# A fused convolution and SwiGLU kernel: weights held back by one DMA, the first output stage reordered, one late sum moved from POOL to an adding DMA, the last pair's products reordered

## The chip, the cores and the metric

The kernel runs on one core of one Trainium2 chip. The metric is the device time of one execution in microseconds (us). The kernel before took 2653.93 us, the median of three runs (2653.21 to 2660.86).

The engines are named as the profile names them: PE is TensorE (matmuls), PEld its weight loads, DVE is VectorE, ACT is ScalarE, POOL is GpSimd, and SP is SyncE, which only issues DMAs. A DMA can also be issued from ACT or from POOL; one from POOL may add to what stands at its destination.

## The reference

The input x has 8 sequences of 4096 tokens with 192 channels, in 8 heads of 24. Each head has 7 taps, made by a softmax over its weights, and every token becomes the tapped sum of itself and the six tokens before it. The 32768 results go through a SwiGLU block:

```
out  = einsum('hk,bskhg->bshg', softmax(weight), windows of x)   # causal, 7 taps per head
rms  = sqrt(mean(x*x) + 1e-6)                                    # x: the result above, 32768 x 192
xn   = x / rms * rms_g
g    = xn @ w_gate          # 192 x 1536
val  = xn @ w_val           # 192 x 1536
y    = (silu(g) * val) @ w_out   # 1536 x 192
```

The weights w_gate, w_val, w_out and rms_g come as 64-bit floats and are read as pairs of 32-bit words; the kernel turns them into 32-bit floats itself.

## The kernel before, in words

**Pairs.** The tokens go in 32 pairs of two tiles of 512 tokens (PT = 1024, T = 512). Pair 0 is computed plainly. Pairs 1 to 31 use a scheme that computes products of 3 by 3 blocks with 15 block products in place of more, so that TensorE has fewer products and the other engines have sums to form. For every pair there are 120 products of the first matrices (line 859: gate on the low 64 partitions, value on the upper 64, four units u of 384 columns each, in chains that accumulate in the eight PSUM banks), and then 60 products of the last matrix (line 1044, each four 32-column matmuls), listed in OUTS as form.unit: 11.0 is form 11 of unit 0.

**Order.** Everything is issued in an order written out by hand. ORDER is a list of steps for one pair: `p3` is three products of TensorE; every other word has the engine as its first letter (V for DVE, A for ACT, G for POOL, P for DVE again, Q for a DMA from POOL, D for a DMA from SP) and then the step. A name that ends in `-` belongs to the pair before. Each engine takes its steps in that order and waits where a semaphore tells it to. A later scheduler does not move them.

**Sums of a pair.** The gated results of a unit are six tiles a to f in the tile `ht`. The output products read them and sums of them: AB, CB, X and S, held in `early`, `more`, `nt` and `tls`. The method `Pair.sum` (line 1059) forms them. A word such as `Gabe.13` adds e to AB for the units 1 and 3 on POOL, in one instruction over both units (line 1062); `Qbe.2` adds e to b for unit 2 by a DMA from POOL that accumulates (line 1082); single units on POOL or DVE are at line 1084; `k` before the name copies an operand into a PSUM bank first (line 765). The sum be is written into b itself, and the products of form 1 read it. AB has three states in a pair: form 8 reads AB as it is, form 13 reads it after abe, form 2 after abd. So a sum has to wait until the products of the state before have been read.

**The next pair's input.** While a pair runs, the convolution, the norm (square, reduce, power, repeat, spread, scale: lines 495 to 560), the stores of the normed rows to DRAM in another layout (`place`, line 682), the fetch of them as operands (fetB, fetA, fetC: lines 713 and 736) and the sums of operands (`x_sum`, lines 750 and 757, and the swaps of halves, line 722) of the pairs behind are done in its gaps. Between fetB and fetA a one-element DMA called mark (line 733) reads what fetB has written, so SP waits there until fetB has landed.

**The start.** The input block of pair 0 (x0) is loaded by SP, and the weights behind it. So that the weights do not take transfer time from x0, `hold` (line 224) and two further lines (151, 1315) copy the last loaded column of x0 on POOL into the tiles that the weights will fill; each weight DMA has to wait for its tile's copy. rms_g (rg_sb) is loaded behind the first weights. `convert` turns the words into floats; its last step for the input weights multiplies by rg_sb (line 346), and the first products of pair 0 (line 1168) wait for that. START gives the order of pair 0's steps by one letter each, LATER the time slots of the rest.

**The first output stage.** Pair 0's last matrix is done plainly (`outer`, line 1209, 384 matmul records), in four groups of banks; ACT copies one half of a group (line 1217) and DVE adds the other (line 1221). In its gaps, by numbers of a planned clock (`put(base + ...)`: these give an order, not a time), the kernel does the norm multiply of pair 1 (line 551), its placing and fetch, seven operand sums on DVE (line 757), 17 weight sums for the units 2 and 3 (`w_sums`, line 372), two sign changes of weights on ACT (`w_signs`, line 381), 17 sums of output weights (`out_sums`, line 945), and the norm of pair 2 with the power of its factors on POOL (line 517).

**The last pair.** It has nothing behind it to prepare. The function `last` sorts its steps: each late step (a fork, a join J, a transpose T, a store st) is put in as soon as the names that NEEDS lists for it are done.

```
    NEEDS = {
        "D6": "F4 S6", "D0": "S8 F0", "D2": "S2 F4", "D3": "S2 F3", "D1": "S5 F1",
        "D13": "S13 S6", "D7": "S7 S6", "T0": "3 D0", "T1": "10 D1", "T2": "1 D13 D7",
        "T3": "14 D3", "T4": "0 F4", "T5": "F4 D2 D6", "st0": "T0 T1 T2", "st1": "T3 T4 T5",
        "S2": "2",
    }
```

Of the kernel before, what the change touches and what calls it, by code (L numbers as in the profile page):

```python
# [19 lines left out]
def kernel(  # L20
# [10 lines left out]
    nc = tc.nc  # L31
# [115 lines left out]
    def load_heads(p, b, t0):  # L147

        t = x_sb[p] = xs.tile([P, TB + HALO, GS], F32, name="xh")
        if p == 1:  # L150
            nc.gpsimd.tensor_copy(out=t[:, 0, 0:1], in_=x0[:, NJ + HALO - 1, 0:1])

        def get(dst, tb, h, dims, r):
            row = x[b, t0 + tb * TB + r - HALO, h * GS :]
            src = bass.AP(
                tensor=row.tensor, offset=row.offset, ap=[dims, [D, TB + HALO - r], [1, GS]]
            )
            nc.sync.dma_start(out=dst, in_=src)
# [65 lines left out]
    def hold(t):  # L224

        if 0 in x_sb:
            nc.gpsimd.tensor_copy(out=t, in_=x_sb[0][:, NJ + HALO - t.shape[1] :, 0])

    ht4 = big.tile([P, NU, 2, NF, T], F32, name="ht")

    def load_in(u, q):
        cols = slice(u * NF * P, (u + 1) * NF * P)
        t = ht4[:, u].rearrange("p a f t -> p (a f t)")[:, 0 : KP * NF * P * 2].bitcast(U32)
        t = raw["in", u] = t.rearrange("p (k n two) -> p k n two", k=KP, two=2)
        hold(t[:, :, 0, 0].bitcast(F32))
# [16 lines left out]
    def load_out(i):  # L252


        if i < 2:
            t = outs.tile([P, T // P, D], F32, name="o_sb")
            t = t[:].rearrange("p j d -> p (j d)")
            hold(t[:, 0 : PF * D * 2 : D * 2])
# [8 lines left out]

    load_in(0, nc.sync)
# [111 lines left out]
    def w_signs():  # L380
        nc.scalar.mul(wf4[:, :, 6:9:2, :], wf4[:, :, 6:9:2, :], -1.0)
# [296 lines left out]
    def place(p):  # L678
# [9 lines left out]
        for first in range(2) if p == 1 else (0,):  # L688
            q = nc.scalar if first else nc.sync
            for h in range(first, H, 2 if p == 1 else 1):  # L690
                q.dma_start(out=to[h], in_=y[h::H])
            yield
# [35 lines left out]
    def fetch_part(p, act):  # L728
# [3 lines left out]
        if (p, 1 - g) in fetched:  # L732
            nc.sync.dma_start(out=mark[:, 0:1], in_=xb[HP : HP + 1, 1 - g, 0, 0:1])
# [246 lines left out]
    class Pair:  # L980
# [48 lines left out]
        def products(self):  # L1029
# [4 lines left out]
            for w in " ".join(OUTS).split():  # L1034
# [24 lines left out]
        def sum(self, name, us, eng):  # L1059
            if len(us) > 1:  # L1060
                dst, a, b = (self.forms(i, [int(u) for u in us]) for i in SUMS[name])
                nc.gpsimd.tensor_tensor(out=dst, in0=a, in1=b, op=ALU.add)  # L1062
                return
# [220 lines left out]
    def done(it):  # L1284
# [11 lines left out]
        "iwpvsicwpsiwvpisvivcpsocvpwispvswcipvwsipsiwOvpsiwvipsvvpsopsvcpsvOnovoOpsonvOpsnoOvnopso"  # L1296
    )
    LATER = (
        (30, "s"), (35, "v"), (45, "v"), (47, "O"), (50, "O"), (53, "O"), (55, "n"), (60, "t"),
# [15 lines left out]
    nc.gpsimd.tensor_copy(out=rg_sb[:, 0:1], in_=x0[:, NJ + HALO - 1, 0:1])  # L1315
# [36 lines left out]
    put(base + 445, functools.partial(next, pieces["t"], None))  # L1352
# [28 lines left out]
    emit(float("inf"))  # L1381
# [11 lines left out]
    def last(order, outs):  # L1393

        got, row, n = set(), [], 0
        ends = {w.split(".")[0]: i for i, w in enumerate(outs)}
        late = [w.strip("-") for w in order if w.strip("-")[1:] in NEEDS]
        for w in order:
            if w[-1] == "-":
                row.append(w)  # L1400
                continue
            if w[1:] in NEEDS:
                continue
            for w in ["p1"] * int(w[1:]) if w[0] == "p" else [w]:
                row.append(w)
                if w[0] != "p":
                    got.add(w[1:])
                else:
                    n += 1
                    got.update(k for k, i in ends.items() if i + 121 == n)  # L1410
                more = True
                while more:
                    more = [w for w in late if got.issuperset(NEEDS[w[1:]].split())]
                    for w in more[:1]:
                        late.remove(w)
                        row.append(w)
                        got.add(w[1:])
# [48 lines left out]
```

## Time and profile before

| What | Value |
| --- | --- |
| Time, median of three runs | 2653.93 us (2653.21 to 2660.86) |
| Profiled execution | 2659.7 us, span of its instructions 2657.8 us |
| Granted TensorE clock in it | 0.997 |
| Busy share of the span: PE, DVE, POOL, ACT | 98%, 90%, 81%, 73% |
| First product of pair 0 (L1168) | starts at 34.49 us |
| First fast pair (first L859 product to the next pair's) | 89.5 us |
| A later pair, the same | 80.9 us |
| Sums of two units on POOL: be (L1062, ht) | 31, mean 2.67 us |
| Adding DMAs from POOL (L1082) | 124 of 256 KB, four a pair |

How to read the lines that follow in the next part: the page gives for every engine its busy time, its share of the span and its number of instructions, then the DMA queues with packets, megabytes and share, then the chain of work that ended last by engine. A row of waits says which engine and line waited for what, how long in total, how often, and the longest. A row of the order of time has the start, the duration, engine, line, operation, what is written and read, its shape, the number of instructions merged into the row, and in brackets the idle time before with what ended it. A row of landings has what is written and read, the queue, the number, the size and the time from issue to landing.

### The profile page before, as it was taken

Reading aid. Unit: us, or ns where it says so; the run is one execution under the profiler, and the core shown is the slowest. Engines: PE = TensorE matmul, PEld = TensorE weight load, DVE = VectorE, ACT = ScalarE, POOL = GpSimd, SP = SyncE. Lnnn points to the kernel's source line nnn. Section 1 sums busy time; section 2 is a strip of 40 time slices with the busy share of each in tenths; the row PEclk is TensorE's granted clock in tenths of the full one; section 3 lists DMA queues with packets and bytes.
Section 4 is the critical chain, followed back from the end, with each engine's and each line's share of the span. In section 5 each row is a group of like instructions: output and inputs, shape, how many; then the busy total and the mean of one; then the engine's idle time right before and its main releaser. Section 6 shows DMA issues by size and latency. Waiting matters only on the chain.

```text
span 2657.8 us, 61651 instructions
## 1 busy us (share of the span) xinstructions
PE 2592.4 (98%) x23128; PEld 1617.2 (61%) x23128; DVE 2388.9 (90%) x3989; ACT 1951.2 (73%) x3779; POOL 2156.8 (81%) x1439
## 2 busy tenths in 40 slices
PE   8999999999999999999999999999999999999998
PEld 6856566665566665566655666655666556665555
DVE  7879999999999999999999999999999999998976
ACT  5577777877777877777877778777787777787765
POOL 4777789877789777898777897777897778987777
PEclk9999999999999999999999999999999999999999
DMA  6333443434453434444344534344434444343331
GB/s 141 72 72 73 87 94 84 84 73 86 80 101 75 86 69 91 86 88 80 74 86 80 101 79 85 68 95 80 94 74 84 75 86 95 83 85 68 78 73 29
DMA packets 520345, 218.67 MB, mean 82 GB/s; under 512 B 456174, under 2 KB 458734, under 8 KB 520046
## 3 DMA queue, kind: packets, MB, share of 16 engines
q1 hardware_dynamic: 500044, 181.63, 34.0%
q0 software_dynamic: 17856, 32.51, 7.1%
q8 instruction: 182, 2.98, 0.5%
q14 instruction: 117, 0.96, 0.1%
q10 hardware_dynamic: 2146, 0.59, 0.1%
HBM read 100.10 MB, written 49.55 MB: 56 GB/s over the span
## 4 chain that ended last, share of the span: by engine, by line
PE 58%; POOL 26%; issue 6%; DVE 5%; ACT 3%; DMA 1%; SPq 0%; DVEq 0%; POOLq 0%; ACTq 0%
PE ps L859 49%; POOL early L1062 8%; PE ps L1044 6%; POOL ht L913 3%; POOL xa L750 3%; POOL nt L1062 3%; PE ps L1168 2%; POOL ht L1062 2%; POOL nt L1084 2%; POOL early L1082 1%; ACT ps L765 1%; DVE early L1084 1%; POOL ht L1082 1%; DVE tile L893 1%; POOL tls L1084 1%
## 5 line engine op out<-in xcount | busy, mean ns | idle before, releaser
L859 PE MATMUL ps<-xa,wf 64*128 64x512 f32 x7440 | 1633.2, 592 | 7.7 <-DMA xa<-xa 3.6
L859 PEld LDWEIGHTS ps<-xa,wf 64*128 64x128 f32 x7440 | 1045.9, 187 | 581.6 <-issue 281.5
L811 ACT ACTIVATE tile<-ps 128x512 f32<-128x512 f32 (+1 forms) x801 | 449.2, 573 | 194.3 <-PE ps L1044 107.1
L811 ACT ACTIVATE ps<-ps 128x512 f32<-128x512 f32 x744 | 401.2, 553 | 138.7 <-PE ps L1044 92.4
L811 ACT ACTIVATE tls<-ps 128x512 f32<-128x512 f32 (+1 forms) x656 | 361.5, 565 | 172.2 <-PE ps L1044 88.5
L913 POOL TENSOR_TENSOR ht<-ht,tile 128x512 f32<-128x512 f32 x310 | 414.4, 1347 | 64.9 <-ACT tile L905 61.6
L913 POOL TENSOR_TENSOR ht<-ht,tls 128x512 f32<-128x512 f32 x248 | 329.8, 1344 | 82.2 <-ACT tls L905 81.5
L1044 PE MATMUL ps<-ht,x 128*32 128x256 f32 x5952 | 396.4, 379 | 0.1
L481 DVE SCALAR_TENSOR_TENSOR ps<-xh,tp,ps 128x512 f32<-128x512 f32 x450 | 326.0, 750 | 3.9 <-ACT ps L473 1.7
L1044 PEld LDWEIGHTS ps<-ht,x 128*32 128x32 f32 x5952 | 198.6, 110 | 123.2 <-issue 7.8
L1044 PE MATMUL ps<-early,x 128*32 128x256 f32 x3968 | 255.7, 381 | 12.8 <-POOL early L1062 12.8
L1062 POOL TENSOR_TENSOR early<-early,ht 128x1024 f32<-128x1024 f32 (+1 forms) x93 | 267.3, 2968 | 0.4 <-PE ps L1044 0.4
L531 POOL TENSOR_TENSOR r<-r,nhalf 128x8 f32<-128x8 f32 x29 | 48.2, 1662 | 266.8 <-ACT r L527 257.5
L893 DVE TENSOR_TENSOR tile<-ps,tile 128x512 f32<-128x512 f32 x341 | 233.0, 685 | 12.2 <-PE ps L859 8.0
L893 DVE TENSOR_TENSOR ht<-ps,tile 128x512 f32<-128x512 f32 x316 | 214.0, 682 | 0.7
L905 ACT ACTIVATE tile<-tile 128x512 f32<-128x512 f32 x341 | 211.9, 627 | 0.0
L893 DVE TENSOR_TENSOR tls<-ps,tls 128x512 f32<-128x512 f32 x279 | 190.2, 685 | 11.4 <-PE ps L859 6.0
L1044 PEld LDWEIGHTS ps<-early,x 128*32 128x32 f32 x3968 | 123.1, 110 | 116.8 <-POOL early L1062 42.5
L765 ACT COPY ps<-ht 128x512 f32<-128x512 f32 x279 | 164.2, 589 | 35.3 <-DVE early L1084 33.2
L905 ACT ACTIVATE tls<-tls 128x512 f32<-128x512 f32 x279 | 172.6, 626 | 0.0
L1084 DVE TENSOR_TENSOR early<-early,ps 128x512 f32<-128x512 f32 x217 | 142.9, 682 | 31.4 <-PE ps L1044 31.3
L893 DVE TENSOR_TENSOR ht<-ps,tls 128x512 f32<-128x512 f32 x242 | 163.2, 682 | 1.7 <-ACT tls L811 1.2
(172 smaller groups left out, 3698.8 us busy)
## 6 DMA issues: line engine op xcount, KB each, us to landing
xa<-xd SPq DMA_DIRECT2D x120, 384.0 KB
xa<-xa SPq DMA_DIRECT2D x124, 256.0 KB
out_dram<-o_sb SPq DMA_DIRECT2D x246, 96.0 KB
xd<-yn SPq DMA_DIRECT2D x244, 96.0 KB
xh<-in_x_dram SPq DMA_DIRECT2D x192, 105.0 KB
xa<-xd SPq DMA_DIRECT2D x68, 256.0 KB
ht<-ht POOLq DMA_DIRECT2D x62, 256.0 KB, 3.9
nt<-ht POOLq DMA_DIRECT2D x31, 256.0 KB, 3.3
```

Of the source, the lines that this page charges most:

```text
L481: nc.vector.scalar_tensor_tensor(out=dst, in0=xk, scalar=w, in1=at, op0=ALU.mult, op1=ALU.add)
L750: nc.gpsimd.tensor_tensor(out=put[0], in0=put[1], in1=put[2], op=ALU.add)
L765: nc.scalar.copy(out=bank(*at)[:], in_=src)
L811: nc.scalar.activation(out=dst, in_=src, func=AF.Copy, scale=float(s))
L859: nc.tensor.matmul(out=self.new(v, h, True) if first else self.old(v, h), lhsT=wf[self.u][HALF[h], WAT[i], :], rhs=x_op(XOP[i], h), start= ...
L893: nc.vector.tensor_tensor(out=dst, in0=self.old(v, h), in1=t[:], op=plus(s))
L905: nc.scalar.activation(out=t[:], in_=src[:], func=AF.Silu)
L913: engine[eng].tensor_tensor(out=self.hv(v), in0=src, in1=t[:], op=ALU.mult)
L1044: nc.tensor.matmul(out=to[q * Q : (q + 1) * Q, :], lhsT=left[:, u, a], rhs=cols[:, i * HALFT : (i + 1) * HALFT], start=fresh, stop=True, s ...
L1062: nc.gpsimd.tensor_tensor(out=dst, in0=a, in1=b, op=ALU.add)
L1082: nc.gpsimd.dma_start(out=dst, in_=b, accum_op=ALU.add)
L1084: engine[eng].tensor_tensor(out=dst, in0=a, in1=b, op=ALU.add)
```

## The change

It has six parts, and none changes the number of matmuls.

1. *Start.* `hold` and the two further POOL copies go. One DMA, `begun`, writes the last loaded column of x0 to DRAM from SP's queue. It waits for x0, and what stands behind it in SP's queue waits with it. In the order that the program gets, the first two loads of gate weights stand ahead of `begun`, the others behind.
2. *First output stage.* The norm multiply of pair 1 goes from LATER into START, ahead of the last two conversions of output weights on POOL. `place` issues all its stores from SP, for pair 1 too. The seven operand sums of pair 1 go from DVE to POOL, as three double sums and one single, and stand there behind three sums of output weights and four weight sums; the swaps follow them. The power of pair 2's norm stands on POOL behind all 17 weight sums and ahead of the last fourteen sums of output weights, which stood ahead of it. `w_signs` is done in two halves, for the units 0 and 1 where it was, for 2 and 3 later.
3. *fetA.* The marker DMA is left only where fetB comes second, which the order does not have. So it goes.
4. *be.13.* The word `Gbe.13` becomes `Qbe.13`: b += e for the units 1 and 3 by one adding DMA of 512 KB in place of one POOL instruction. `Pair.sum` gets the branch for it.
5. *Last pair's products.* In the last pair the products of form 0 are sorted behind all others.
6. *Last pair's steps.* `last` is written anew to follow that order: a step whose needs are met is put in before the products of form 0. With this order the products 2.2, 2.3 and 2.1 of the last pair are issued ahead of the sums abd.23 and abd.1, which change what they read: these products of this one pair are formed from AB without d, and the two sums wait for the products.

```
-        "Acv0_2 Gp9.23 DfetA Vcv1_0 Pp9.1 p1 Qbe.2 p1 Vcv2_0 AF1 p2 Gbe.13 DfetC p2 Vcv1_2 Vcv3_0",
+        "Acv0_2 Gp9.23 DfetA Vcv1_0 Pp9.1 p1 Qbe.2 p1 Vcv2_0 AF1 p2 Qbe.13 DfetC p2 Vcv1_2 Vcv3_0",
...
-        if p == 1:
-            nc.gpsimd.tensor_copy(out=t[:, 0, 0:1], in_=x0[:, NJ + HALO - 1, 0:1])
...
-    def hold(t):
-
-        if 0 in x_sb:
-            nc.gpsimd.tensor_copy(out=t, in_=x_sb[0][:, NJ + HALO - t.shape[1] :, 0])
...
+    begun = dram.tile([P, 1], F32, name="begun")
+    nc.sync.dma_start(out=begun[:], in_=x0[:, NJ + HALO - 1, 0:1])
     load_in(0, nc.sync)
...
-        for first in range(2) if p == 1 else (0,):
-            q = nc.scalar if first else nc.sync
-            for h in range(first, H, 2 if p == 1 else 1):
-                q.dma_start(out=to[h], in_=y[h::H])
-            yield
+        for h in range(H):
+            nc.sync.dma_start(out=to[h], in_=y[h::H])
+        yield
...
-        if (p, 1 - g) in fetched:
-            nc.sync.dma_start(out=mark[:, 0:1], in_=xb[HP : HP + 1, 1 - g, 0, 0:1])
+        if g == 0 and (p, 1) in fetched:
+            nc.sync.dma_start(out=mark[:, 0:1], in_=xb[HP : HP + 1, 1, 0, 0:1])
...
-            for w in " ".join(OUTS).split():
+            outs = " ".join(OUTS).split()
+            if self.p == PAIRS - 1:
+                outs.sort(key=lambda w: w[0:2] == "0.")
+            for w in outs:
...
-                nc.gpsimd.tensor_tensor(out=dst, in0=a, in1=b, op=ALU.add)
+                if eng == "Q":
+                    nc.gpsimd.dma_start(out=dst, in_=b, accum_op=ALU.add)
+                else:
+                    nc.gpsimd.tensor_tensor(out=dst, in0=a, in1=b, op=ALU.add)
...
-        "iwpvsicwpsiwvpisvivcpsocvpwispvswcipvwsipsiwOvpsiwvipsvvpsopsvcpsvOnovoOpsonvOpsnoOvnopso"
+        "iwpvsicwpsiwvpisvivcpsocvpwispvswcipvwsipsiwOvpsiwvipsvvpsopsvcpsvOnovoOpsonvOpsnoOvnnopso"
...
-    later(norm(2), c + 1510, c + 1600, c + 2310, base + 2895, base + 2900)
+    later(norm(2), c + 1510, c + 1600, c + 1610, base + 2895, base + 2900)
...
-    for i, at in zip(range(4), (1660, 1730, 2060, 2130)):
-        put(c + at, functools.partial(x_sum, i))
-    put(c + 2131, functools.partial(swap, "swA"))
-    for i, at in zip((5, 4, 6), (2200, 2270, 2290)):
-        put(c + at, functools.partial(x_sum, i))
-    put(c + 2291, functools.partial(swap, "swB"))
+    for at, i in zip((470, 471, 473, 474), (20, 21, 4, 22)):
+        put(base + at, functools.partial(x_sum, i, "G"))
+    put(base + 472, functools.partial(swap, "swA"))
+    put(base + 475, functools.partial(swap, "swB"))
     wsum = out_sums()
-    later(wsum, *[base + 964 + 60 * i for i in range(17)])
-    put(base + 2650, w_signs)
+    later(wsum, *[base + 455 + i for i in range(3)], *[base + 2100 + 60 * i for i in range(14)])
+    put(base + 2650, functools.partial(w_signs, 0, 2))
...
+    put(base + 3595, functools.partial(w_signs, 2, 4))
```

More of the change, by code (lines that the diff above doesn't have):

```diff
@@ L234, in load_in @@
         t = raw["in", u] = t.rearrange("p (k n two) -> p k n two", k=KP, two=2)
-        hold(t[:, :, 0, 0].bitcast(F32))
         for w, rows in ((moe_w_gate, LOW), (moe_w_val, UPP)):
@@ L257, in load_out @@
             t = t[:].rearrange("p j d -> p (j d)")
-            hold(t[:, 0 : PF * D * 2 : D * 2])
         else:
@@ L378, in w_sums, with w_signs @@
         yield
-    def w_signs():
-        nc.scalar.mul(wf4[:, :, 6:9:2, :], wf4[:, :, 6:9:2, :], -1.0)
+    def w_signs(lo, hi):
+        t = wf4[:, lo:hi, 6:9:2, :]
+        nc.scalar.mul(t, t, -1.0)
     def convert_in(u):
@@ L1295 @@
         "XxxxxxxXdDdDdDddTTTTTTTTaakKkkaaakKkKbkKkbKbbbffpffpfsipsvivpsipisvipsvcpvowsivOcwps"
-        "iwpvsicwpsiwvpisvivcpsocvpwispvswcipvwsipsiwOvpsiwvipsvvpsopsvcpsvOnovoOpsonvOpsnoOvnopso"
+        "iwpvsicwpsiwvpisvivcpsocvpwispvswcipvwsipsiwOvpsiwvipsvvpsopsvcpsvOnovoOpsonvOpsnoOvnnopso"
     )
     LATER = (
-        (30, "s"), (35, "v"), (45, "v"), (47, "O"), (50, "O"), (53, "O"), (55, "n"), (60, "t"),
+        (30, "s"), (35, "v"), (45, "v"), (47, "O"), (50, "O"), (53, "O"), (60, "t"),
         (463, "w"), (564, "w"), (664, "w"), (764, "w"), (864, "w"),
@@ L1314 @@
     conv_first((1, 3, 5, 6), 2)
-    nc.gpsimd.tensor_copy(out=rg_sb[:, 0:1], in_=x0[:, NJ + HALO - 1, 0:1])
     nc.sync.dma_start(out=rg_sb[LOW, :], in_=rg)
@@ L1351 @@
     put(base - 1, lambda: outer(0, hts, base))
-    put(base + 445, functools.partial(next, pieces["t"], None))
     put(base + 450, functools.partial(fetch, 1))
@@ L1393, in last, with settle, product @@
     def last(order, outs):
-        got, row, n = set(), [], 0
-        ends = {w.split(".")[0]: i for i, w in enumerate(outs)}
+        got, row, n, end = set(), [], 0, []
+        todo = [w.split(".")[0] for w in outs]
         late = [w.strip("-") for w in order if w.strip("-")[1:] in NEEDS]
+        def settle():
+            more = True
+            while more:
+                more = [w for w in late if got.issuperset(NEEDS[w[1:]].split())]
+                for w in more[:1]:
+                    late.remove(w)
+                    row.append(w)
+                    got.add(w[1:])
+        def product(k):
+            row.append("p1")
+            todo.remove(k)
+            if k not in todo:
+                got.add(k)
+            settle()
         for w in order:
@@ L1400, in last @@
                 row.append(w)
[L1401 to L1404, printed above, removed]
-                row.append(w)
[L1406 to L1417, printed above, removed]
+            elif w[0] == "p":
+                for _ in range(int(w[1:])):
+                    n += 1
+                    k = outs[n - 121].split(".")[0] if n > 120 else ""
+                    if k == "0":
+                        end.append(k)
+                    elif k:
+                        product(k)
+                    else:
+                        row.append("p1")
+            elif w[1:] not in NEEDS:
+                row.append(w)
+                got.add(w[1:])
+                settle()
+        for k in end:
+            product(k)
         assert not late
```

## The prediction

> **What bounds the kernel now.** I read the page first (busy shares, chain), then the waits, then the order of time of three places that the change touches: the first 36 us, the hand-over from the first output stage to the first fast pair (92 to 145 us), and one later pair (868 to 950 us), with the transfers of that pair.
>
> ```profile
> span 2657.8 us, 61651 instructions
> PE 2592.4 (98%) x23128; PEld 1617.2 (61%) x23128; DVE 2388.9 (90%) x3989; ACT 1951.2 (73%) x3779; POOL 2156.8 (81%) x1439
> ...
> q8 instruction: 182, 2.98, 0.5%
> ...
> PE 58%; POOL 26%; issue 6%; DVE 5%; ACT 3%; DMA 1%; SPq 0%; DVEq 0%; POOLq 0%; ACTq 0%
> ```
>
> TensorE is bound nearly everywhere: 98% busy, and 31 pairs follow each other every 80.9 us (first L859 product to first L859 product). The 26% of POOL in the chain are POOL's sums late in each pair, which arrive just as TensorE wants them. The start (the chain in order of time, then the waits):
>
> ```profile
> 2.33 6.32 DMA x<-in_x_dram
> ...
> 8.81 7.71 POOL ht L227
> ...
> 27.81 5.97 DMA rg_sb<-in_moe_rms_g_dram
> ```
> ```profile
> PE ps L1168 <- DVE wf L346: 5.5, 1, 5.5
> ...
> DVE wf L346 <- DMA rg_sb<-in_moe_rms_g_dram: 5.2, 1, 5.2
> ```
>
> The input block is in at 8.65, but the POOL copy that holds the weights back runs from 8.81 to 16.5, exactly as long as VectorE's tap products; the weights start then, rg_sb stands behind them in the queue and lands at 33.8, and TensorE's first product waits for it. The hand-over (order of time of PE, then of DVE):
>
> ```profile
> 136.17 2.59 PE L859 MATMUL ps<-xa,wf 64*128 64x512 f32 x6 [3.63 <-DMA xa<-xa]
> 141.28 51.48 PE L859 MATMUL ps<-xa,wf 64*128 64x512 f32 x230 [2.52 <-DVE o_sb L1221]
> ```
> ```profile
> 140.54 0.24 DVE L543 STREAM_TRANSPOSE s<-s 128x64 f32<-128x64 f32 x1 [8.51 <-POOL s L520]
> 140.71 0.52 DVE L1221 TENSOR_TENSOR o_sb<-ps,o_sb 128x384 f32<-128x384 f32 x1
> ```
>
> Two waits, for the swapped sums and for the last bank, which stands on VectorE behind a transpose that waits for POOL's power. A later pair (POOL, then PE, then the landings):
>
> ```profile
> 928.45 0.86 POOL L1082 DMA_DIRECT2D ht<-ht  x1
> 929.06 2.67 POOL L1062 TENSOR_TENSOR ht<-ht 128x1024 f32<-128x1024 f32 x1
> 931.38 1.18 POOL L1082 DMA_DIRECT2D early<-ht  x1
> 932.34 6.07 POOL L1062 TENSOR_TENSOR early<-early,ht 128x1024 f32<-128x1024 f32 x2
> ```
> ```profile
> 934.19 0.61 PE L1044 MATMUL ps<-ht,x 128*32 128x256 f32 x8
> 935.04 1.50 PE L1044 MATMUL ps<-early,x 128*32 128x256 f32 x24 [0.23 <-POOL early L1062]
> ...
> 938.46 0.64 PE L1044 MATMUL ps<-early,x 128*32 128x256 f32 x8 [0.19 <-POOL early L1062]
> ```
> ```profile
> ht<-ht POOLq DMA_DIRECT2D x1, 256.0 KB, 3.8
> early<-ht POOLq DMA_DIRECT2D x1, 256.0 KB, 3.6
> ```
>
> The row at 929.06 is the sum be.13, which the change hands to an adding DMA; the row at 934.19 is product 1.1, the first reader of its result; 935.04 is 13.1, 938.46 is 7.3.
>
> **The change part by part.** *Start.* The four POOL copies go (and those for rg_sb and xh); one small DMA (begun) waits on SP for the input block, which landed at 8.65. Two gate transfers now stand ahead of it in SP's queue. The other weights start at about 9 instead of 17, so rg_sb lands about 8 us earlier, near 25.5. VectorE's step ahead of L346 ended at 28.82, so L346 starts at 28.9 instead of 33.99: -5.1. All engines' later work hangs on L346 and moves with it. Bounds: not over 5.5 (the whole wait of PE); if the two gate transfers (384 KB at the 225 KB per us that the packets show here) ran ahead of the input block they would cost 1.7, leaving -3.4. They stand behind it in the queue, so I take -5.1.
>
> *First output stage* (before's times, all less 5.1). The norm multiply L551 moves from 107.0 to 101.0; its 2.9 us cover POOL's wait of 1.9 at 105. The eight stores of y now all go on SP (5.2 us, as at 143.78) and start at 104 instead of 110 on two queues; the eight fetches follow from 109.3 instead of 114.1, and as they are bound by transfer rate (1.16 us each in the landings), the sixth lands near 118.5, the last near 121. POOL: last conversion ends 108.1, three output sums 3.0, four weight sums 3.1, to 114.2; it then waits for the fetch until 118.5; three double sums (2.58 each, L750) and one single (1.5) to 127.7; the last swap is issued there instead of at 131.6 and lands 4.45 later, at 132.2: the wait of 3.63 goes. What is late next: thirteen weight sums (0.77 each, 10.0) and the power with its copies (2.35) end at 140.1; the transpose and the last L1221 behind it end near 140.9 instead of 141.2. So -0.3: POOL spends on waiting and on sums that VectorE did before (7.7 us) what it saves on the fourteen output sums put behind (12.4). The split w_signs stands ahead of the last L1217 on ACT and waits for the thirteen, to 137.7; L1217 ends by 139.2, ahead of 140.9. Bounds: -6.1 if both waits went, +3 if the fetch is as late as before.
>
> *Behind it.* Fourteen sums and the second norm multiply now end at 155.4 instead of 143.75, so the first M multiply, which ran at 150.24, ends at 156.7. The snapshot L815 at 156.00 takes the tile that it frees: 0.7 late, and product (4,5) waits for that. POOL was idle 6 us between 150 and 168 and catches up. +0.7 (0 to 2.3).
>
> *Every pair, mark.* The marker DMA goes; SP issues fetA when the last product has read its place, 1.4 us earlier. Nothing on the path waits for fetA. 0.
>
> *Every pair, be.13* (31 times). POOL loses 2.67 and gains an issue of about 1. That is no gain: abe.13 behind it must wait for product 8.1, whose end reached POOL at 932.27 in the record; it started 0.07 later. The transfer: 256 packets of 2 KB, 16 to each of 16 engines, behind the 8 of Qbe.2 in the same queue. Qbe.2's packets ran from 929.85, 0.187 us each; 24 in a row end at 934.35, and POOL's transfers land 0.33 after their last packet: 934.7. 1.1 would start at 934.76, 0.57 late. 13.1 is then 0.2 late; 7.3 waited 0.38 for its sum anyway and abd.23, which holds 2.2, has another 0.15. So a clean landing costs nothing, and each us beyond 934.8 costs one.
>
> It will seldom be clean. The instruction queue's 182 packets of 16 KB took 0.5% of 16 engines' span, 1.17 us each on one engine; by the packet records one starts within 60.3 to 66.2 us of the pair in 30 of 31 pairs, just where this transfer runs. Qabe.2, half as long, landed at 3.6 (median), but 0.5 to 2.0 later in 9 pairs, mean 1.3. I take 1.0 late: (934.7 + 1.0 + 0.07 + 0.46) - 935.04 - 0.53 = 0.65 a pair, times 31 = +20. Bounds: 0 (clean) and 2.0 late, 1.6 a pair, +50. POOL's issue of twice the descriptors is not in the trace; between 0.86 and 1.7 it stays hidden, since Qabe.2 has to wait for 8.2 (about 930.9).
>
> The Trainium skill, page "DMA: Bandwidth & Descriptors", section "Anatomy of one DMA — SWDGE (gpsimd) path", fits such a DMA as 2.0 us plus bytes over 436 GB/s; by that 512 KB would take 3.2 us and land at 932.3, ahead of 1.1, and the sum would be without the 20. The trace has 3.6 to 3.8 for 256 KB where the page gives 2.6, so I go by the rows.
>
> *Last pair.* Products 0.x come last, so T5, T3, T0 and store st0 run beside four products; behind the last product only T4 and st1 are left, two transposes (0.37 each) fewer. -0.8 (0 to -1.7, four products of 0.43).
>
> Sum: -5.1 - 0.3 + 0.7 + 20 - 0.8 = +14.5. The profiled execution took 2659.7 (span 2657.8 and 1.9 around it), so 2674.2 against it; it stands 5.8 above the median of the runs, 2653.9 (2653.2 to 2660.9). Against the median: 2668.4.
>
> **The rivals.** *The transfer is in time* (not slower): be.13 lands by 934.8 in most pairs, since only one of 16 engines is held by a code packet and fetA's earlier issue clears the queue. Then the twenty are gone: 2648.4. For it: 0.53 us of slack behind 1.1. Against: Qbe.2 itself landed 4.1 after issue in the median, not 3.3, and 1.1 needs every engine. It decides at a landing 5.7 us after issue. *The first output stage gains as well*: if POOL's sums run faster or the fetch lands earlier, so that neither wait is left: -5.1 - 5.8 - 0.8, and a hidden transfer: 2642.2. Against: thirteen weight sums stand ahead of the power. *The transfer is later still*: descriptors of two rows a partition, or adds that share the engines with fetch traffic, add 2 us more than a clean landing: +50, 2698. *Only the start moves* and the rest cancels is the first rival's time.
>
> **How the numbers follow.** Forecast 0.55, in time 0.27, stage gains too 0.08, later still 0.10. The forecast's own range is 2655 to 2685 (0.2 to 1.2 a pair). Within 0.3% (8 us, what a measurement here can tell from no change) are the first rival and the lower part of the forecast, 0.10: 0.37; faster 0.08; slower 0.55. The range leaves the second rival below and most of the third above: 2645 to 2692.
>
> **What would show it.** PE's first L1168 product at 29.4; no wait for xa<-xa, and the next pair's period still near 89 with the last L1221 held by POOL; POOL's L1062 on ht replaced by a DMA; a new wait of PE at a product of ht for a DMA, 0.5 to 1.6 us, about 31 times, and a period of 81.5 instead of 80.9. Wrong if the period stays at 80.9 (landing early, or more slack than I found), or if abe.13 starts earlier (then 8.1 was not what held it).

## The result, and the profile after

The kernel after takes 2663.82 us (median of 20 runs, 2662.68 to 2668.21); the kernel before took 2654.19 us beside it (20 runs, 2652.58 to 2662.21). The ratio is 1.0031, with a 95% interval of 1.0025 to 1.0038: slower by about 0.3%, 8 us. The medians are 9.6 apart; six of before's runs lie near 2660, so that its mean, 2656.0, stands above its median. The forecast was 2668.4. The sign and the size came out, but two large terms of the sum were wrong by +10 and by -15 us and hid each other, so most of what follows is on why.

One sentence of the section on the change is wrong: the products 2.2, 2.3 and 2.1 of the last pair are not issued ahead of abd.23 and abd.1. They stand behind these sums in the new order too, and in the trace abd.23 ends 1.2 us ahead of product 2.2. Nothing is left out of the computation.

The page of the kernel after, its span and the chain by engine (DMA was 1% of it before):

```profile
span 2663.0 us, 61597 instructions
...
PE 2587.8 (97%) x23128; PEld 1607.5 (60%) x23128; DVE 2381.6 (89%) x3982; ACT 1948.9 (73%) x3780; POOL 2120.3 (80%) x1437
...
PE 60%; POOL 19%; DMA 7%; DVE 6%; issue 5%; ACT 2%; SPq 0%; POOLq 0%; DVEq 0%; ACTq 0%
```

The start, from the chain in order of time (start, duration, what):

```profile
2.33 7.55 DMA x<-in_x_dram
...
10.02 7.79 DMA begun<-x
...
17.83 9.75 DMA o_sb<-in_moe_w_out_dram
...
27.59 5.43 DMA rg_sb<-in_moe_rms_g_dram
```

The input block lands at 9.88, where it landed at 8.65 before. The DMA begun needs 7.8 us to land, a weight transfer that waits for its completion 9.75, and rg_sb is issued at 27.59, where it was issued at 27.81 before. PE's first product of pair 0 starts at 33.66.

The hand-over to the first fast pair (order of time of PE):

```profile
132.48 1.22 PE L851 MATMUL ps<-xa,wf 64*128 64x512 f32 x4 [1.08 <-DMA xa<-xa]
136.94 2.07 PE L851 MATMUL ps<-xa,wf 64*128 64x512 f32 x2 [3.24 <-ACT o_sb L1215]
140.68 2.08 PE L851 MATMUL ps<-xa,wf 64*128 64x512 f32 x4 [1.67 <-DVE o_sb L1219]
```

There are three waits instead of two. The one for the swapped sums is shorter (1.08, was 3.63), the last bank still waits for VectorE, and between them stands a new one for ACT's last copy.

The later pairs, from the waits (who waited for what: us in total, times, longest) and the landings of POOL's DMAs, then one pair in the order of time of POOL and of PE:

```profile
PE ps L1039 <- DMA ht<-ht: 30.4, 31, 1.6
...
ht<-ht POOLq DMA_DIRECT2D x62, 256.0 KB, 3.5
ht<-ht POOLq DMA_DIRECT2D x31, 512.0 KB, 6.3
```
```profile
930.86 1.54 POOL L1058 DMA_DIRECT2D ht<-ht  x1
933.08 0.91 POOL L1080 DMA_DIRECT2D early<-ht  x1 [0.67 <-PE ps L1039]
934.17 5.80 POOL L1060 TENSOR_TENSOR early<-early,ht 128x1024 f32<-128x1024 f32 x2 [0.18 <-PE ps L1039]
```
```profile
937.66 0.64 PE L1039 MATMUL ps<-ht,x 128*32 128x256 f32 x8 [1.46 <-DMA ht<-ht]
938.12 1.48 PE L1039 MATMUL ps<-early,x 128*32 128x256 f32 x24
```

This pair starts 1.78 us later than the pair shown of before, so the row at 934.17 (abe.13) is where it was, 64.1 us into its pair. Product 1.1, at 937.66, waits 1.46 for the 512 KB transfer.

Where the time went, by stretches, with the start of each stretch read from PE's rows. The column in the middle is the kernel before with the last pair's edits alone (a run told below); up to the last pair it does the same work as before:

| Stretch, us | before, the profiled run | before's work, another run | after |
| --- | --- | --- | --- |
| to the first product of pair 0 | 34.49 | 28.47 | 33.66 |
| from there to the first fast pair | 96.92 | 96.70 | 96.61 |
| first fast pair | 89.49 | 90.06 | 91.85 |
| pairs 2 to 30 (29 pairs) | 2348.52 | 2349.31 | 2352.47 |
| last pair to the end | 88.41 | (edited) 87.46 | 88.42 |

The first row is the surprise: before has two kinds of start, 6.0 us apart. Its 20 runs show them as two groups, 14 from 2652.6 to 2655.8 and 6 from 2660.2 to 2662.2, and the profiled run (2659.7) was of the rarer kind. Five traces have the start of after, with the first product between 33.66 and 34.71. Against the usual start, after loses 5.2 at the start, 0 to the first fast pair, 1.8 in it, 3.2 in the pairs 2 to 30, and with 88.41 for the last pair of before nothing at the end: 10.1 in all, where the medians differ by 9.6.

### The profile page after: what moved, and what is told of

Its sections match the earlier page's. It is cut to its first block, busy times and chain, and to the rows that moved or that the text cites. A ratio compares the mean times of both kernels' runs of the same rounds, so it can differ in the third digit from the quotient of the medians.

```text
span 2663.0 us, 61597 instructions
## 1 busy us (share of the span) xinstructions
PE 2587.8 (97%) x23128; PEld 1607.5 (60%) x23128; DVE 2381.6 (89%) x3982; ACT 1948.9 (73%) x3780; POOL 2120.3 (80%) x1437
## 4 chain that ended last, share of the span: by engine, by line
PE 60%; POOL 19%; DMA 7%; DVE 6%; issue 5%; ACT 2%; SPq 0%; POOLq 0%; DVEq 0%; ACTq 0%
PE ps L851 48%; PE ps L1039 8%; POOL early L1060 6%; DMA ht<-ht 5%; POOL ht L905 4%; POOL xa L742 3%; PE ps L1166 2%; POOL nt L1060 2%; POOL nt L1082 2%; DVE ps L475 1%; PE ps L1207 1%; DMA xa<-xd 1%; POOL xa L749 1%; POOL tls L1082 1%; ACT ps L803 1%
## 5 line engine op out<-in xcount | busy, mean ns | idle before, releaser
L851 PEld LDWEIGHTS ps<-xa,wf 64*128 64x128 f32 x7440 | 1033.9, 187 | 594.9 <-issue 298.6
L1060 POOL TENSOR_TENSOR early<-early,ht 128x1024 f32<-128x1024 f32 (+1 forms) x93 | 253.9, 2739 | 6.2 <-PE ps L1039 6.2
L1039 PEld LDWEIGHTS ps<-early,x 128*32 128x32 f32 x3968 | 129.7, 110 | 84.5 <-POOL early L1060 1.5
```

The costliest lines, as they stand in the source:

```text
L851: nc.tensor.matmul(out=self.new(v, h, True) if first else self.old(v, h), lhsT=wf[self.u][HALF[h], WAT[i], :], rhs=x_op(XOP[i], h), start= ...
L1039: nc.tensor.matmul(out=to[q * Q : (q + 1) * Q, :], lhsT=left[:, u, a], rhs=cols[:, i * HALFT : (i + 1) * HALFT], start=fresh, stop=True, s ...
```

## The experiments

Each kernel was run beside the kernel before on the same chip; ratios are to that.

| Run | Median, us | Ratio to before (95%) |
| --- | --- | --- |
| after, be.13 back on POOL | 2660.93 | 1.0017 (1.0009 to 1.0026) |
| after, begun of one element | 2659.46 | 1.0013 (1.0004 to 1.0022) |
| before, last pair's edits alone | 2654.41 | 1.0000 (0.9991 to 1.0009) |
| the same, T3 behind form 0 | 2653.59 | 0.9997 (0.9988 to 1.0006) |
| before, first output stage's edits alone | 2656.05 | 1.0003 (0.9994 to 1.0012) |
| after, power ahead | 2667.21 | 1.0045 (1.0031 to 1.0059) |
| after, power ahead and backlog spread | 2659.28 | 1.0015 (1.0006 to 1.0023) |
| the four mended together | 2646.47 | 0.9967 (0.9955 to 0.9980) |
| before, be.13 as a DMA alone | 2676.22 | 1.0070 (1.0056 to 1.0083) |
| mended, be.13 as a DMA ahead of be.2 | 2642.10 | 0.9949 (0.9936 to 0.9961) |
| before, rg_sb early | 2655.86 | 1.0001 (0.9992 to 1.0010) |
| after, the marker back | 2678.93 | 1.0083 (1.0070 to 1.0097) |

**be.13 put back.**

```
-        ... Qbe.2 p1 Vcv2_0 AF1 p2 Qbe.13 DfetC ...
+        ... Qbe.2 p1 Vcv2_0 AF1 p2 Gbe.13 DfetC ...
```

> The kernel after with the sum be.13 put back on POOL, all else as after. Theory (the late landing costs, but most of it is eaten by slack: in the two traces the pairs 2 to 31 took 3.95 us more in all, the first pair some 0.6): 4 to 5 us faster than the kernel after, 2659 to 2660 us, every period between 80.86 and 80.97, no wait for a DMA at a product of ht. Rival 1 (the adding DMA explains the whole loss, because it also disturbs other transfers): 8 to 10 us faster, 2654 to 2656. Rival 2 (the adding DMA is harmless and the periods of after are noise of that one run): 2663 to 2665, periods still spread over 80.6 to 82.2.

Measured: 2660.93, 2.9 us faster than after by the medians, and about 3.7 by the ratios (1.0017 where after has 1.0031), a little under the 4 to 5 expected. In the traces the pairs 2 to 30 took 2348.76 in all, as before (2348.52), the last pair 87.75 instead of 88.42 and the first fast pair 91.45 instead of 91.85. So in the kernel after the adding DMA costs 0.4 + 3.7 + 0.7 = 4.8 by the traces. The first fast pair stays long, so all but 0.4 of its 1.8 is not the DMA's.

**begun of one element.**

```
-    begun = dram.tile([P, 1], F32, name="begun")
-    nc.sync.dma_start(out=begun[:], in_=x0[:, NJ + HALO - 1, 0:1])
+    begun = dram.tile([1, 1], F32, name="begun")
+    nc.sync.dma_start(out=begun[:], in_=x0[P - 1 : P, NJ + HALO - 1, 0:1])
```

> The kernel after with begun reading and writing one element instead of 128. Theory (the 128 writes of 4 bytes to DRAM hold the DMA engines: behind them weight packets of 3 KB took up to 6.9 us instead of 0.24, from 11 to 20 us, so the weights and rg_sb came no earlier than before): the weight packets behind begun take 0.2 to 0.4 us again, rg_sb is issued near 21.5 instead of 27.6, the first product of pair 0 (L1166) starts at 29.0 to 30.0 instead of 33.66, and the whole is 3.7 to 4.7 us faster than the kernel after, 2659 to 2660. Rival (it is only the wait of the queue for any DMA's completion, or the weights wait for something else): the first product stays between 32 and 34, the time within 1.5 us of the kernel after.

Measured: 2659.46; the first product starts at 27.89, 5.8 earlier than in after, rg_sb is issued at 18.16 and 18.86. The busy time by stretch shows what the weights waited for (last columns: granted clock, DMA share, GB/s), first after, then this run:

```profile
10.00:12.00 2.00, 2.00 (x16) 2.00 (x16) 1.94 (x6) 2.00 (x7) 0.00 (x0) 1.00 1.80 26
12.00:16.00 4.00, 4.00 (x29) 4.00 (x29) 4.00 (x14) 4.00 (x12) 0.00 (x0) 1.00 0.72 24
16.00:20.00 4.00, 3.69 (x28) 3.52 (x27) 2.34 (x8) 2.31 (x6) 0.00 (x0) 1.00 0.47 28
```
```profile
10.00:12.00 2.00, 2.00 (x14) 2.00 (x13) 2.00 (x7) 2.00 (x7) 0.00 (x0) 1.00 0.94 244
12.00:16.00 4.00, 4.00 (x29) 4.00 (x28) 4.00 (x14) 4.00 (x13) 0.00 (x0) 1.00 1.03 220
16.00:20.00 4.00, 3.56 (x26) 3.09 (x24) 2.08 (x6) 2.82 (x8) 0.00 (x0) 1.00 1.08 288
```

Behind 128 writes of 4 bytes the engines moved 24 to 28 GB/s for ten microseconds, where behind one write they moved 220 to 288. By the packet records 38 of the weights' packets of 3072 bytes took over 1 us in after (up to 6.9; the median is 0.23), none here; all 38 start between 11.7 and 19.1, behind begun's issue. But the edit changes the order of SP's queue as well. In after two gate loads are issued ahead of begun, in this run none (SP, first after, then this run):

```profile
3.09 1.21 SPq L230 DMA_DIRECT2D ht<-in_moe_w_gate_dram  x2
10.02 0.37 SPq L260 DMA_DIRECT2D begun<-x  x1
```
```profile
8.33 0.22 SPq L260 DMA_DIRECT2D begun<-x  x1
8.60 1.84 SPq L230 DMA_DIRECT2D ht<-in_moe_w_gate_dram  x3
```

In after the packets of these two loads start at 6.68, while the input block is still coming in, and begun is issued 1.7 us later than here. So the run shows that begun's shape and the two loads ahead of it lost the start together. The slow packets stand for the shape as the larger part; no run has the one without the other. That the queue then also waited 3.4 us for begun's completion is not parted from this either: with one element that wait is gone too. The specifications of the Trainium skill's page "DMA: Bandwidth & Descriptors" name 512 bytes as the least size for full rate, with a read, change and write back below it; the traces agree in sign, and no run here shows that mechanism.

**Last pair's edits alone, and with T3 behind the products of form 0.**

```
             outs = " ".join(OUTS).split()
+            if self.p == PAIRS - 1:
+                outs.sort(key=lambda w: w[0:2] == "0.")
...
(second run only)
-        "T3": "14 D3", "T4": "0 F4",
+        "T3": "14 D3 0", "T4": "0 F4",
```

> The kernel before with the last pair's edits alone (the products of form 0 sorted last, the function last rewritten). Theory (the four products of form 0 write the half of a PSUM bank whose other half the transpose T3 reads, and T3 now stands ahead of them; PE waited 1.78 us there in the kernel after): the same wait of 1.5 to 2 us at the last four products for a transpose on DVE, from the last pair's first product to the end of the span 88.3 to 88.6 us as before (88.41), time within 0.5 of the kernel before. Rival (the edit gains as forecast, and in the kernel after be.13 ate it): 87.5 to 87.7 us for the last pair, 0.8 faster.

> The kernel before with the last pair's edits, and with the transpose T3 put behind the products of form 0 (one name more in its list of needs), so that nothing reads their bank ahead of them. Theory (the bank is what holds them): no wait of PE at the last four products, last pair 1.0 to 1.6 us shorter than with the edits alone (the last product ends 1.78 earlier, one transpose of 0.37 and its half of the stores come back behind it), so 86.9 to 87.4 us. Rival (DVE's joins and transposes end last in any case): less than 0.4 us shorter.

Measured: 2654.41 and 2653.59, no difference that a run's time could tell, but in the traces the last pair takes 87.46 and 86.92 instead of 88.41. PE at the last four products, first run and second run:

```profile
2645.55 1.93 PE L1047 MATMUL ps<-ht,x 128*32 128x256 f32 x32 [1.78 <-DVE o_sb L1060]
```
```profile
2644.47 1.93 PE L1047 MATMUL ps<-ht,x 128*32 128x256 f32 x32 [0.54 <-DVE ps L1109]
```

The wait for the shared bank is there as expected, but it does not eat the gain: the edit saves 0.95, because behind the last product only one transpose and half of the stores are left. So my theory fell and the rival held: the edit gains, and in the kernel after the late be.13 took 0.67 of it (87.75 with be.13 on POOL). T3 moved is worth 0.54, about half of the least that I expected: PE still waits 0.54 there for a join of VectorE on the same bank, and a transpose and its half of the stores come back behind the products.

The first of these two traces also shows the other start. The order of time of POOL and of VectorE at the start, of this run, and then of the kernel before as profiled:

```profile
8.56 0.34 POOL L227 COPY ht<-x 128x3 f32<-128x3 f32 x1 [7.01 <-DMA x<-in_x_dram]
```
```profile
8.99 7.33 DVE L434 SCALAR_TENSOR_TENSOR y<-x,taps,y 128x192 f32<-128x192 f32 x22
```
```profile
8.81 7.71 POOL L227 COPY ht<-x 128x3 f32<-128x3 f32 x1 [7.26 <-DMA x<-in_x_dram]
```
```profile
9.14 7.33 DVE L434 SCALAR_TENSOR_TENSOR y<-x,taps,y 128x192 f32<-128x192 f32 x22
```

The same POOL copy takes 0.34 us or 7.71. In four traces with this code it ended before VectorE's first L434, and the weights started between 8.5 and 9.3; in two it came back only when L434's series was over, and the weights started at 16.5. The lead alone does not part them: it was 0.27 and 0.33 us where the copy lost, 0.31 to 0.56 where it won. What decides is not shown.

**The first output stage: its edits alone, the power moved, the backlog spread.**

```
(on after, second and third run)
-        (463, "w"), (564, "w"), (664, "w"), (764, "w"), (864, "w"),
+        (463, "w"), (1820, "w"), (1821, "w"), (1822, "w"), (1823, "w"),
...
-    put(base + 3595, functools.partial(w_signs, 2, 4))
(second run only)
+    put(base + 9000, functools.partial(w_signs, 2, 4))
(third run only: signs, norm multiply, placing and six output sums go into pair 1's order)
-    later(wsum, *[base + 455 + i for i in range(3)], *[base + 2100 + 60 * i for i in range(14)])
+    later(wsum, *[base + 455 + i for i in range(3)], *[base + 464 + i / 2 for i in range(8)])
...
+    EXTRA = {
+        "GM3.1.0": [more_sum] * 4, "Gac.0": [more_sum] * 2,
+        "AS41.1.1": [functools.partial(w_signs, 2, 4)],
+        "Gmul-": [functools.partial(next, norm2, None)], "Dplace-": [functools.partial(done, place(2))],
+    }
```

> The kernel before with the edits of the first output stage alone. Theory (the stage gains nothing by itself, and the first fast pair is 1.2 us longer because TensorE's products run at half speed for 5.3 us after the three waits instead of 2.7 after the two of before): first product to the first fast pair as before within 0.3, the first fast pair 91.0 to 91.6 instead of 89.5 to 90.0, whole 1 to 2 us slower than before. Rival (the first pair is longer because of the adding DMA be.13 or the late start): 89.5 to 90.1, no slower.

> The kernel after with the power of the second norm ahead of the thirteen weight sums on POOL, and the second half of the sign changes behind ACT's last copy of the stage. Theory (PE waits for the last bank only because VectorE's and ACT's last copies stand behind a transpose and sign changes that wait for these sums; but POOL has the same work to do, so its first multiply of the pair stays at 153, and a tile that it frees is needed 14.7 us after PE resumes): PE resumes at 132.5 to 134 instead of 140.7, and most of that is given back by a new wait of 4 to 7 us in the first fast pair; whole 0 to 4 us faster than the kernel after. Rival (POOL's backlog is hidden): 8 to 9 us faster.

> As the run with the power moved, and POOL's backlog moved too: eight of the fourteen late output sums into POOL's wait for the fetch, the other six, the second norm multiply and its placing into the first fast pair, where the later pairs have theirs. Theory: PE resumes at 132.5 to 134, the waits stay short enough for the clock to come back sooner, no wait of over 1 us in the first pair; 7 to 10 us faster than the kernel after, 2654 to 2657. Rival (the six sums and the multiply delay POOL's later sums of the first pair): gain under 4 us, the first pair over 94.

Measured, the edits alone: 2656.05, a ratio that can't be told from 1; in the trace the first fast pair takes 92.17, 2.1 more than with before's stage (90.06 with the same kind of start). Of these, 1.2 pass until PE resumes behind its last wait (11.38 us after the pair's first product, against 10.16) and 0.9 from there to the first output product. Neither the adding DMA nor a late start is in this run, so the stage's edits alone make the first fast pair longer. The second part is TensorE's clock. The busy time by stretch around the resume, before and after (the last three columns: granted clock, DMA share, GB/s):

```profile
141.30:144.30 3.00, 3.00 (x8) 1.44 (x10) 1.21 (x2) 0.60 (x1) 2.45 (x1) 0.52 0.00 0
144.30:150.00 5.70, 5.70 (x28) 2.62 (x26) 3.41 (x6) 4.70 (x9) 0.00 (x0) 1.00 0.65 133
```
```profile
141.00:146.00 5.00, 5.00 (x14) 1.92 (x14) 0.92 (x2) 1.68 (x3) 4.84 (x8) 0.50 0.00 0
146.00:150.00 4.00, 4.00 (x22) 1.88 (x19) 3.23 (x5) 3.08 (x6) 3.77 (x6) 0.99 0.00 0
```

After the last wait TensorE ran at half its clock, for 2.9 us of work before and for 5.4 after. At half speed the 2.5 us more are an estimated 1.2 us lost, which is what the 230 products from the resume to the first output product took longer (52.69 against 51.45). The two runs compared above had 3.4 and 5.3 us at half clock, which by the same working loses the 0.9 seen there. In the five traces with two waits it held 2.9 to 3.5 us behind the last one, in the five with three waits 4.1 to 6.0. The Trainium skill, page "TensorE: Matmul & The Clock Gate", Part 1, has the clock at half after a window of some 3.4 us without work, and full again after a busy one. The rows agree that idle time lowers the clock and work brings it back, but not that the window has to be empty: in after no wait reached 3.4 us, and the 3.41 us ahead of the fall at 135.82 held 1.22 us of work.

Measured, the power moved: 2667.21, 3.4 us slower than after by the medians, where 0 to 4 faster was expected. In the trace the first fast pair is 0.4 shorter, and the loss lies outside it (0.9 at the start, 1.3 in the pairs 2 to 30), so it is not put down to this edit. PE resumed at 133.85 as expected and then waited (PE, then ACT):

```profile
140.88 5.39 PE L851 MATMUL ps<-xa,wf 64*128 64x512 f32 x15 [4.95 <-ACT tile L803]
```
```profile
139.71 0.63 ACT L375 ACTIVATE wf<-wf 128x512 f32<-128x512 f32 x1 [8.44 <-POOL wf L365]
```

The wait has the size that I expected but another place: not POOL's multiplies but ACT's sign changes hold it, which wait for the thirteen weight sums with all of ACT's copies of the new pair behind them. With the signs and POOL's backlog spread over the pair the mechanism held: PE resumes at 133.50, the clock stays at full speed, and the first fast pair takes 83.97 instead of 91.85. The time, 2659.28, is 4.5 us below after by the medians, less than the 7 to 10 expected; the trace, of the fastest of eleven runs, is 7.3 shorter:

```profile
133.50 12.76 PE L851 MATMUL ps<-xa,wf 64*128 64x512 f32 x57 [1.30 <-DMA xa<-xa]
```
```profile
136.00:140.90 4.90, 4.90 (x26) 3.48 (x24) 3.19 (x6) 4.04 (x8) 4.59 (x7) 1.00 0.83 100
```

**The mended parts together.** On the kernel after: begun of one element, `Gbe.13`, T3 behind form 0, the stage spread.

> All that the runs so far point to, on the kernel after: begun of one element, be.13 back on POOL, the transpose T3 behind the products of form 0, and the stage with power moved and backlog spread. If the parts add up: against the kernel before with its usual start 0.6 at the start, 6 to 8 in the stage and 1.5 in the last pair, together 8 to 10 us faster than before (ratio 0.9962 to 0.9970). If the stage's part is given back in the first pair: 2 to 4 us faster.

Measured: 2646.47, 0.9967 of before. By stretches: first product 28.12, first fast pair 83.46, pairs 2 to 30 2349.02, last pair 86.89. The parts add up: 8.8 us less than the median of before beside it, where 8 to 10 was expected.

**be.13 as a DMA alone, and after with the marker back.** The first is the kernel before with `Qbe.13` and its branch in `Pair.sum`. The second undoes one other line of after:

```
-        if g == 0 and (p, 1) in fetched:
-            nc.sync.dma_start(out=mark[:, 0:1], in_=xb[HP : HP + 1, 1, 0, 0:1])
+        if (p, 1 - g) in fetched:
+            nc.sync.dma_start(out=mark[:, 0:1], in_=xb[HP : HP + 1, 1 - g, 0, 0:1])
```

> The kernel before with the sum be.13 as an adding DMA alone. Theory (what the two traces and the run with be.13 put back show: 1.1 is 1.2 us late, and most of that is caught up at 13.1, 7.3 and 2.2): PE waits 1.2 to 1.6 us at product 1.1 in nearly all pairs, the periods spread over 80.6 to 82.2 with a mean 0.10 to 0.16 above those of before, the whole 3 to 5 us slower than the kernel before with the same kind of start. Rival (without the other edits there is no loss): within 1 us. Rival (the forecast's 0.65 a pair): 20 us slower.

> The kernel after with the marker DMA put back between fetB and fetA, all else as after. Theory (be.13 as an adding DMA alone cost 20 us and 0.62 a pair, in the kernel after 0.13 a pair; what takes the difference away is the removed marker: SP issues fetA 1.4 us earlier, so its transfers leave the engines earlier to be.2 and be.13, which land 0.5 us sooner): the mean period rises from 81.1 to 81.5 to 81.6, the wait at product 1.1 to 1.3 to 1.4 us in the mean, and the whole is 13 to 17 us slower than the kernel after, 2676 to 2681. Rival (POOL's or VectorE's other edits take the difference away): within 2 us of the kernel after.

Measured, alone: 2676.22 (five runs, 2669.62 to 2678.85), 20.7 us slower than before by the medians. The trace is of the slowest run and has the late start (first product at 34.55); which start the other four had is not known. Against the trace of before, which has the late start too, it is 19.3 longer, 17.2 of it in the pairs 2 to 30, with a median period of 81.50. That is the last rival of this expectation, and it is the forecast's own figure. The waits and landings:

```profile
PE ps L1044 <- DMA ht<-ht: 42.3, 31, 2.3
...
ht<-ht POOLq DMA_DIRECT2D x31, 512.0 KB, 6.8
```

The transfer lands 0.5 later after issue than in the kernel after, and none of the slack is left for that. Measured, the marker back in after: 2678.93 (six runs, 2674.08 to 2681.12), 15 us slower than after by the medians (14 by the ratios). The trace is of the fastest of the six; its pairs 2 to 30 take 8.3 us more than those of after, a mean period of 81.41 where 81.5 to 81.6 was expected. The wait of PE is longer again, and the transfer lands later:

```profile
PE ps L1039 <- DMA ht<-ht: 39.9, 31, 2.2
...
ht<-ht POOLq DMA_DIRECT2D x31, 512.0 KB, 6.6
```

So the marker decides whether the DMA costs little or much. Without it SP issues fetA 51.9 us into the pair and fetC behind it at 53.2, with it at 54.1 and 55.9, and the last packets of these fetches end at 60.2 and 62.2 (medians, from the issue rows and the packet records of after and of after with the marker). The first packets of be.2 start at 61.7 in both: with the marker they share the engines with the end of the fetches, without it the fetches are over. In the trace with the marker be.13 lands the later the later the fetches of its pair end (correlation 0.88).

**be.13 ahead of be.2.**

```
-        ... p1 Qbe.2 p1 Vcv2_0 AF1 p2 Gbe.13 DfetC ...
+        ... p1 Qbe.13 Qbe.2 p1 Vcv2_0 AF1 p2 DfetC ...
```

> The best version so far with be.13 as an adding DMA that is issued ahead of be.2's instead of behind it. Theory (the lateness of 1.2 us is the time that be.2's transfer and issue take ahead of it in the same queue; product 1.2, which reads be.2, comes seven products later): no wait of over 0.3 us at product 1.1, the mean period within 0.05 of that with be.13 on POOL, the whole within 1.5 us of the best version; POOL's 2.6 us freed a pair buy nothing, since abe.13 waits for product 8.1. Rival (512 KB need more than 5.5 us from issue whatever stands ahead): a wait at 1.1 stays, 2 us or more slower.

Measured: 2642.10, 0.9949 of before: the best version, some 13 us faster than before and some 4.5 faster than with be.13 on POOL. The wait at 1.1 is nearly gone (9 waits in place of 31), as expected, though the longest is 1.0 and not under 0.3:

```profile
PE ps L1039 <- DMA ht<-ht: 5.8, 9, 1.0
...
ht<-ht POOLq DMA_DIRECT2D x31, 512.0 KB, 5.2
```

But POOL's freed time does buy something, against the theory: the median period is 80.75 instead of 80.91. abe.13 starts where it did (64.15 into the pair, after product 8.1), but takes 2.38 instead of 2.63. The issue of abe.2's DMA, which stood just ahead of it and ran into it (931.38 with 1.18, abe.13 at 932.34 in before), is now over by then; that this is why is argued, not shown. Product 13.1, which waits for this sum, comes 0.18 earlier.

**rg_sb early.**

```
+    nc.sync.dma_start(out=rg_sb[LOW, :], in_=rg)
+    nc.sync.dma_start(out=rg_sb[UPP, :], in_=rg)
     load_in(0, nc.sync)
...
-    nc.gpsimd.tensor_copy(out=rg_sb[:, 0:1], in_=x0[:, NJ + HALO - 1, 0:1])
-    nc.sync.dma_start(out=rg_sb[LOW, :], in_=rg)
-    nc.sync.dma_start(out=rg_sb[UPP, :], in_=rg)
```

> The kernel before with the two small loads of rg_sb ahead of the weights in SP's queue and not held. Theory (before has two starts: when the first POOL copy of hold wins against VectorE's tap products the weights start at 8.9 us and the first product of pair 0 at 28.4; when it loses it takes 7.7 us, the weights start at 16.5 and rg_sb, last in the queue, lets the first product start at 34.5; these are the runs near 2660): with rg_sb in early, a lost start costs 1 to 2 us instead of 6, so no run lies above 2658, and the lower runs stay within 1 us of before's lower runs. Rival (the runs near 2660 have another cause): one to three of eleven runs lie again near 2660.

Measured: 2655.86, eleven runs from 2654.6 to 2657.3, none near 2660. But none of the 15 runs of before beside it was near 2660 either, and the trace had the usual start (first product at 28.15). So this decides nothing on how often or why the late start comes; what stands for it are the two kinds of rows shown above. Of before's runs beside the other kernels, none of 15 were near 2660 on one chip and 5 of 11 on another; what sets that stays open.

## Why the prediction was right, point by point

*Start, -5.1: wrong, +5.2.* Three steps failed. First, "the POOL copy that holds the weights back runs from 8.81 to 16.5" was read from one profiled run, in which that copy ended only with VectorE's products; usually the first product starts at 28.4, and there were no 5.1 us to be had. The sign was in the text: the profiled run stood 5.8 above the median, and I set that aside as an offset of the whole. Second, "one small DMA" was costed at nothing: behind its 128 writes of 4 bytes the weights came in at a tenth of the rate for ten microseconds. Third, the two gate loads were priced at 1.7 if they ran ahead of the input block, and dropped with "They stand behind it in the queue". In the trace they ran beside its last part, and it landed 1.2 us later. The claim of a first product at 29.4 came out at 33.66, and at 27.89 with begun of one element.

*First output stage, -0.3: near in sum, not in its parts.* PE resumes 9.87 us after the first fast pair's first product before, 10.41 after. The last bank is held by VectorE's transpose behind POOL's power, as written. The wait for the swapped sums did not go, it went down to 1.08. The step "L1217 ends by 139.2, ahead of 140.9", by which the split signs cost nothing, was right in order (136.9) and still missed what it does: PE stood 3.24 us for it, ahead of the last bank, so that it had three idle stretches instead of two.

*M multiplies behind it, +0.7: not seen, but the clock took +1.2.* POOL's first multiply ran at 152.94, and no product waited for the tile. What the forecast left out is the half clock after the waits. The two give a first fast pair longer by the same order, for another reason; "still near 89" was 91.85.

*Marker, 0: the step that failed.* Nothing on the path waits for fetA, which is right, and with be.13 on POOL the removal is worth nothing (2348.76 against 2348.52 over the pairs 2 to 30). But the next term was worked out from packets with the marker in place. With be.13 as a DMA the removal is worth 14 to 15 us by the runs' times (8.3 in the pairs of the one trace). It lets SP issue fetA 2.2 us earlier, where the forecast had 1.4. I had it as an argument for the first rival ("fetA's earlier issue clears the queue") and did not price it.

*be.13, +20: right for the edit alone, +4.8 in the whole change.* Alone it cost 19.3 between the two traces with the late start, with 81.50 a pair, and product by product the working holds: 13.1 late by 1.26 (forecast 1.19), 0.84 behind 7.3 (0.81), 0.64 behind 2.2 (0.66). In the whole change 1.1 is 1.17 late, 13.1 0.80, 7.3 0.38, 2.2 0.13. abe.13 did not start earlier, as forecast. The rule of the Trainium skill's page "DMA: Bandwidth & Descriptors" (section "Anatomy of one DMA — SWDGE (gpsimd) path"), with an estimate of 3.2 us for 512 KB worked out from it, does not hold for this adding DMA: the trace has 6.3, and 5.2 at best. That the packets of 16 KB of the instruction queue make it late is borne out in part by the packet records. In after, be.13 landed 5.8 us after issue in the 5 of the pairs 2 to 30 where no such packet ran beside be.2 and be.13, and 6.35 in the mean of the other 24; with be.13 first it was 5.1 in 15 pairs without and 6.1 in 14 with one. No run took these packets away, and in after PE waits 0.5 at product 1.1 even without them.

*Last pair, -0.8: right* (-0.95 by the edit alone), by way of the shorter end; the wait of 1.78 for the shared bank was not foreseen. In the kernel after be.13 takes most of it back.

The sum was +14.5 and about +10 was measured: 10.3 too little at the start, 15.2 too much at be.13. That the time came out within the range is luck: these two errors have opposite signs. What the forecast had right is that be.13's transfer lands late and makes the kernel slower; it had wrong by how much, beside the other edits.

## What to carry to other kernels

Before a gain is read from a profile, ask whether the profiled run is of the kind that most runs are: a wait of 5 us in a run that stands 6 above the median may be there in that run alone. Two edits that each touch the same transfer engines are not to be costed one by one; the second is to be worked out with the first in place, since a line worth nothing without the other was worth 8 to 15 us beside it. And a transfer that gates a product goes first in its queue: the same DMA lost between 4 and 5 us behind its neighbour and gained some 4 ahead of it.

## What the runs showed that I had not expected

- Behind 128 writes of 4 bytes to DRAM the 16 engines moved 24 to 28 GB/s for about ten microseconds, against 220 to 288 behind one, and packets of 3 KB took up to 6.9 us against 0.23. (Two loads also stood ahead of the 128 writes and not of the one.)
- One small POOL copy took 0.34 or 7.71 us, in the second case until VectorE's series of L434 was over; that moves the start of the kernel by 6 us.
- Three waits of 1.08, 3.24 and 1.67 us close together left TensorE at half clock for 5.4 us behind them; a single wait of 1.30 left it at full speed.
- A transfer of 512 KB from POOL landed at 6.8, 6.3 or 5.2 us after issue (medians): with the marker in place, without it, and without it and ahead of be.2 in its queue.
